# Loaded tiles with head rows 256 B apart, and their loads shared out over two issuing queues

## The chip, the cores and the metric

One core of a Trainium2 chip. The time is device microseconds of the whole program, a median over executions. A run also leaves a trace of one profiled execution; its span is about 2 us shorter than the time. Each execution lists the clock granted to TensorE; a run is called slow where it lies over 1.5% above the fastest of its kernel.

## The reference, cut to what matters

```python
# q, k, v, alpha: (4, 8, 768, 48) float32
for t in range(S):
    state = alpha[:, :, t, :, None] * state + np.einsum('bhd,bhe->bhde', k[:, :, t], v[:, :, t])
    y[:, :, t] = np.einsum('bhd,bhde->bhe', q[:, :, t], state)
x = y.transpose(0, 2, 1, 3).reshape(B * S, H * D)        # (3072, 384)
out = np.maximum(x @ w1, x @ w2) @ w_out                  # w1, w2: (384, 1024), w_out: (1024, 384)
```

The sequence is worked in 24 chunks (4 batches of 6) of 128 steps. A chunk needs four loads, alpha, k, q and v: 8 heads x 128 steps x 48 float32, so 1024 rows of 192 B (192 KB) each.

## The kernel before

```python
    ldp = ctx.enter_context(tc.tile_pool(name="ldp", bufs=8))
    ...
    def load(i):
        b, c = divmod(i, NCH)
        t = {}
        for name, src in (("af", alpha), ("kf", k), ("qf", q), ("vf", v)):
            t[name] = ldp.tile([128, H, D], FP32, tag=name, name=name)
            nc.sync.dma_start(out=t[name], in_=src[b, :, c * C : (c + 1) * C, :].rearrange("h p d -> p h d"))
        loads[i] = t

    load(0)
    load(1)
    ...                                        # w2f, wof, w1f: three weights of 1.5 MB, also nc.sync
    def gla(i):                                # one chunk; cut to the start of its chain
        nc.scalar.activation(out=lg[:, :, 0:D], in_=t["af"], func=ACTF.Ln)
        nc.gpsimd.tensor_copy(out=vd, in_=t["vf"])
        nc.tensor.matmul(csv, lhsT=mrec, rhs=lg[:, :, 0:D], start=True, stop=True)     # cs
        nc.scalar.activation(out=Em, in_=csv, func=ACTF.Exp, scale=-1.0)
        nc.scalar.activation(out=Ep, in_=csv, func=ACTF.Exp)
        nc.gpsimd.tensor_mul(out=kn[:, :, 0:D], in0=t["kf"], in1=Em)
        nc.vector.tensor_mul(out=qn[:, :, 0:D], in0=t["qf"], in1=Ep)
        ...                                    # transposes of kn, qn; qk, pp, pt, yp; xt by ScalarE
    for i in range(NI):
        if i + 2 < NI:
            load(i + 2)
        gla(i)
        if i == 1:
            weights()                          # ScalarE casts w2h; wq matmuls; w12
        if i % 2 == 1 and i // 2 - LAG >= 0:
            moe(i // 2 - LAG)                  # hp, gT, op; ScalarE evicts and issues the store
```

A scheduler orders the instructions of each engine when the program is built; ScalarE's 174 instructions, TensorE's 1544 matmuls and the issues of each queue come in the built order. It also hands out completion semaphores for the transfers: eight, in turn, whichever queue issues. The built program lets a transfer be issued only when the one eight places before it in that order has landed.

Of the kernel before, what the change touches and what calls it, by code (L numbers as in the profile page):

```python
# [9 lines left out]
FP32 = mybir.dt.float32  # L10
# [5 lines left out]
def kernel(  # L16
# [20 lines left out]
    nc = tc.nc  # L37
    B, H, S, D = q.shape
    C = 128
# [3 lines left out]
    P64 = 64  # L43
# [9 lines left out]
    ldp = ctx.enter_context(tc.tile_pool(name="ldp", bufs=8))  # L53
# [8 lines left out]
    def load(i):  # L62
        b, c = divmod(i, NCH)
        t = {}
        for name, src in (("af", alpha), ("kf", k), ("qf", q), ("vf", v)):
            t[name] = ldp.tile([128, H, D], FP32, tag=name, name=name)
            nc.sync.dma_start(out=t[name], in_=src[b, :, c * C : (c + 1) * C, :].rearrange("h p d -> p h d"))
        loads[i] = t

    load(0)  # L70
    load(1)
    w2f = wp.tile([128, ND, DFF], FP32)
    wof = wp.tile([128, NF, DM], FP32)
# [21 lines left out]
    for n in range(NB):  # L95
        for lst, nm in ((LG, "lg"), (QN, "qn"), (KN, "kn")):
            t = constp.tile([128, H, P64], FP16, name=f"{nm}{n}")
            nc.gpsimd.memset(t, 0.0)
            lst.append(t)
        t = constp.tile([128, 128 + H * VS], FP16, name=f"vp{n}")  # L100
# [3 lines left out]
    for n in range(3):  # L104
        t = constp.tile([128, 128 + HP * SS], FP16, name=f"sb{n}")
# [164 lines left out]
# [5 lines that stand above are left out]
            weights()  # L275
        if i % 2 == 1 and i // 2 - LAG >= 0:
            moe(i // 2 - LAG)
# [32 lines left out]
```

## Time and profile before

| | before |
|---|---|
| time, median | 187.52 us first; 188.06 with the run beside the changed kernel |
| TensorE busy, mean clock | 145.4 us of a 185.5 us span, 0.99 |
| ScalarE busy | 73.8 us (40%) |
| loads | 98304 packets of 192 B, all by SyncE |
| start of kn, chunks 0, 1, 2, 4, 7, 16, 23 | 10.3, 19.7, 32.4, 45.8, 63.8, 124.5, 168.6 us |

The start of kn (GpSimd's product of k and Em), read for each chunk from the timeline, is one number per chunk. From chunk 7 to 23 the pace before is (168.57 - 63.84)/16 = 6.55 us.

### The profile page before, as it was taken

The page shows a single profiled execution, that of the slowest core. Times are in us where ns is not written, and L with a number is a line of the kernel's source. Part 1 is how long each engine was busy: PE and PEld are TensorE (multiplying, and loading weights), DVE is VectorE, ACT ScalarE, POOL GpSimd, SP SyncE. Part 2 cuts the span into 40 slices and gives each one's busy share as a digit, 9 for nine tenths or more (in the row PEclk, how much of TensorE's full clock was granted, in tenths as well). Part 3 has the DMA queues.
Part 4 walks back from the last instruction along what each step waited for, and adds up shares of the span by engine and source line. Part 5 has one row for each costly group of instructions (what it writes and reads, how often), then busy time and mean ns, then how long its engine had stood idle before and what let it go on. Part 6 is the DMA issues. An engine that isn't in the chain of part 4 may idle for free. (4 is left out here: it accounts for less than half of the span.)

```text
span 185.5 us, 3954 instructions
## 1 busy us (share of the span) xinstructions
PE 145.4 (78%) x1544; PEld 101.6 (55%) x1544; DVE 102.6 (55%) x175; ACT 73.8 (40%) x175; POOL 75.9 (41%) x129
## 2 busy tenths in 40 slices
PE   0025779779887898896997878888878988969991
PEld 0024637556555666564675555566556665646760
DVE  4122765782764962955926757717649529559220
ACT  3306306525454616426344443252455163253331
POOL 8950730661464245436512543523633353355000
PEclk9999969999999999999999999999999999999999
DMA  6999999999699599996999994997920020020022
GB/s 119 189 351 378 370 189 169 196 187 168 163 201 216 114 191 206 190 189 142 185 161 221 205 208 105 194 189 157 169 88 0 4 85 2 5 85 0 4 85 85
DMA packets 104963, 28.57 MB, mean 154 GB/s; under 512 B 100080, under 2 KB 104176, under 8 KB 104944
## 3 DMA queue, kind: packets, MB, share of 16 engines
q1 hardware_dynamic: 101680, 23.60, 73.7%
q10 hardware_dynamic: 3264, 4.72, 7.4%
q8 instruction: 12, 0.20, 0.5%
q14 instruction: 7, 0.06, 0.1%
HBM read 23.59 MB, written 4.72 MB: 153 GB/s over the span
## 5 line engine op out<-in xcount | busy, mean ns | idle before, releaser
L171 POOL TENSOR_TENSOR kn<-kf,Em 128x384 f16<-128x384 f32 x24 | 23.9, 995 | 79.2 <-ACT Em L167 59.4
L260 PE MATMUL op<-wo,gT 128*128 128x384 f16 x192 | 40.6, 326 | 0.0
L246 PE MATMUL hp<-xt,w 128*128 128x256 f16 x288 | 38.9, 272 | 1.7 <-ACT xt L236 1.1
L221 DVE TENSOR_TENSOR pt<-pp,u 128x512 f16<-128x512 f32 x48 | 30.9, 685 | 6.2 <-PE pp L219 5.7
L253 DVE TENSOR_SCALAR gT<-hp 128x512 f16<-128x512 f32 x24 | 16.4, 684 | 24.1 <-PE hp L246 24.0
L246 PEld LDWEIGHTS <-w 128*128 128x128 f16 x288 | 26.1, 97 | 5.9 <-issue 3.2
L172 DVE TENSOR_TENSOR qn<-qf,Ep 128x384 f16<-128x384 f32 x24 | 21.1, 878 | 14.1 <-ACT Ep L168 10.6
L232 PE MATMUL yp<-pt,vp 128*128 128x128 f16 x240 | 26.3, 223 | 1.1 <-DVE pt L221 0.8
L177 PE MATMUL tp<-ident,kn 128*128 128x128 f16 x96 | 10.7, 229 | 19.5 <-POOL kn L171 19.5
L263 ACT COPY outs<-op 128x384 f32<-128x384 f32 x24 | 11.5, 480 | 33.6 <-PE op L260 33.5
L181 DVE COPY qk<-tp 128x1024 f16<-128x1024 f16 x24 | 16.5, 689 | 14.3 <-PE tp L177 12.9
L260 PEld LDWEIGHTS <-gT 128*128 128x128 f16 x192 | 16.9, 97 | 9.9 <-issue 1.8
L251 ACT ACTIVATE gT<-hp 128x512 f16<-128x512 f32 x24 | 14.4, 602 | 18.3 <-PE hp L246 18.2
L194 POOL TENSOR_TENSOR sb<-tm,dd 64x192 f16<-64x192 f32 x40 | 20.3, 506 | 2.9
L177 PEld LDWEIGHTS <-kn 128*128 128x128 f16 x96 | 6.1, 100 | 26.0 <-POOL kn L171 26.0
L232 PEld LDWEIGHTS <-vp 128*128 128x128 f16 x240 | 18.2, 100 | 3.3 <-issue 0.2
L167 ACT ACTIVATE Em<-cs 128x384 f32<-128x384 f32 x24 | 11.8, 493 | 18.8 <-PE cs L161 18.8
L236 ACT CAST xt<-yp 128x384 f16<-128x384 f32 x24 | 11.5, 479 | 18.6 <-PE yp L232 17.3
L154 POOL CAST vp<-vf 128x384 f16<-128x384 f32 x24 | 13.1, 550 | 12.6 <-PE yp L232 9.1
L232 PE MATMUL yp<-qk,sb 128*128 128x128 f16 x120 | 16.8, 222 | 1.0 <-POOL sb L194 1.0
L258 PE MATMUL op<-w2o,xt 128*128 128x384 f16 x72 | 16.9, 325 | 0.0
L209 DVE TENSOR_TENSOR tm<-kv,sb 64x192 f32<-64x192 f32 x32 | 11.3, 352 | 5.7 <-POOL sb L194 5.0
(46 smaller groups left out, 161.4 us busy)
## 6 DMA issues: line engine op xcount, KB each, us to landing
af<-in_alpha_dram SPq DMA_DIRECT2D x24, 192.0 KB, 4.5
kf<-in_k_dram SPq DMA_DIRECT2D x24, 192.0 KB, 4.6
qf<-in_q_dram SPq DMA_DIRECT2D x24, 192.0 KB, 4.6
vf<-in_v_dram SPq DMA_DIRECT2D x24, 192.0 KB, 4.6
out_dram<-outs ACTq DMA_DIRECT2D x12, 384.0 KB, 3.4
w2f<-in_moe_w_dram SPq DMA_DIRECT2D x1, 1536.0 KB, 7.3
wof<-in_moe_w_out_dram SPq DMA_DIRECT2D x1, 1536.0 KB, 10.5
w1f<-in_moe_w_dram SPq DMA_DIRECT2D x1, 1536.0 KB, 14.0
```

The source lines that it names most:

```text
L171: nc.gpsimd.tensor_mul(out=kn[:, :, 0:D], in0=t["kf"], in1=Em)
L172: nc.vector.tensor_mul(out=qn[:, :, 0:D], in0=t["qf"], in1=Ep)
L177: nc.tensor.transpose(tp[:, n, j, :], src[:, 2 * j : 2 * j + 2, :].rearrange("p h w -> p (h w)"), ident)
L181: nc.vector.tensor_copy(out=qk, in_=tp)
L194: nc.gpsimd.tensor_mul(out=sd[r, :, e], in0=tm[r], in1=dd[r, :].unsqueeze(2).to_broadcast([64, HP, D]))
L221: nc.vector.tensor_mul(out=pt[:, a], in0=pa[a], in1=u16.unsqueeze(1).to_broadcast([128, HP, C]))
L232: nc.tensor.matmul(yp[:, ds, :], lhsT=l, rhs=r, start=(n == 0), stop=(n == len(mms) - 1))
L246: nc.tensor.matmul(hp[:, n, :], lhsT=w12[:, ds, f * 128 : (f + 1) * 128], rhs=xt[:, ds].rearrange("p n t -> p (n t)"), start=(ds == 0), st ...
L251: nc.scalar.activation(out=gT[:, 2 * f2 : 2 * f2 + 2, :], in_=hp, func=ACTF.Relu)
L253: nc.vector.tensor_relu(out=gT[:, 2 * f2 : 2 * f2 + 2, :], in_=hp)
L258: nc.tensor.matmul(op, lhsT=xt[:, ds, n, :], rhs=w2o[:, ds, :], start=(ds == 0), stop=False)
L260: nc.tensor.matmul(op, lhsT=gT[:, f, n * C : (n + 1) * C], rhs=wo16[:, f, :], start=False, stop=(f == NF - 1))
```

## The change

Its intent: runs of 192 B that begin 256 B apart instead of packed, and half of the issues taken from SyncE.

```diff
-            t[name] = ldp.tile([128, H, D], FP32, tag=name, name=name)
-            nc.sync.dma_start(out=t[name], in_=src[b, :, c * C : (c + 1) * C, :].rearrange("h p d -> p h d"))
+            t[name] = ldp.tile([128, H, P64], FP32, tag=name, name=name)[:, :, 0:D]
+            eng = nc.sync if name in ("af", "qf") else nc.scalar
+            eng.dma_start(out=t[name], in_=src[b, :, c * C : (c + 1) * C, :].rearrange("h p d -> p h d"))
```

## The prediction

> **What bounds the kernel now.** I read the shares by slice first, then busy time by stretches of time, then the waits, and last the timeline of the first 32 us and the SyncE queue's own timeline. Busy time by stretch (columns: us, busy us of each engine with its instruction count, granted clock, mean share of the DMA engines, GB/s):
>
> ```profile
> 0.00:31.40 31.40, 14.72 (x128) 10.60 (x129) 13.96 (x27) 9.51 (x18) 16.27 (x28) 0.95 1.11 253
> 31.40:60.00 28.60, 24.16 (x272) 16.92 (x271) 16.29 (x28) 13.06 (x33) 13.76 (x24) 1.00 1.16 191
> 60.00:130.00 70.00, 60.75 (x670) 42.28 (x668) 43.17 (x74) 30.21 (x75) 27.98 (x47) 1.00 1.05 176
> ```
>
> After 31.4 us (the first expert matmul, hp) TensorE is busy 84 to 87% of the time, so its in-order stream sets the pace: 130.6 us of its 145.4 us lie there. The first 31.4 us hold only 14.7 us of its work; that ramp is where a faster load could pay. The DMA engines read as full almost throughout, which looks like a bound and is not one after the ramp: the SyncE queue pauses again and again (4 to 5 us at a time) for a store or a free buffer.
>
> The ramp, from the timeline, with the issue to landing time of two weights:
>
> ```profile
> w2f<-in_moe_w_dram SPq DMA_DIRECT2D x1, 1536.0 KB, 7.3
> wof<-in_moe_w_out_dram SPq DMA_DIRECT2D x1, 1536.0 KB, 10.5
> ...
> 7.58 0.96 SPq L75 DMA_DIRECT2D w2f<-in_moe_w_dram  x1
> 8.58 0.50 SPq L76 DMA_DIRECT2D wof<-in_moe_w_out_dram  x1
> 14.94 2.94 ACT L128 CAST w2h<-w2f 128x1024 f16<-128x1024 f32 x3 [6.31 <-DMA w2f<-in_moe_w_dram]
> 19.13 0.49 ACT L167 ACTIVATE Em<-cs 128x384 f32<-128x384 f32 x1 [1.25 <-PE cs L161]
> 20.64 3.07 POOL L133 CAST wo<-wof 128x3072 f16<-128x3072 f32 x1
> 27.86 0.48 ACT L141 CAST w2o<-wq 128x384 f16<-128x384 f32 x1 [6.63 <-PE wq L137]
> 31.44 1.25 PE L246 MATMUL hp<-xt,w 128*128 128x256 f16 x10
> ```
>
> Eight row loads, then w2f (landed 14.9), wof (19.1), w1f (23.1); ScalarE casts w2f, then does chunk 1's Em at 19.13; the product wq and w2o follow. So the ramp is made of DMA arrival and of ScalarE's program order.
>
> After the ramp ScalarE is not busy (40% of the span), but it starts every chunk:
>
> ```profile
> POOL kn L171 <- ACT Em L167: 59.4, 16, 8.0
> PE tp L177 <- POOL kn L171: 19.5, 21, 6.2
> ACT Em L167 <- PE cs L161: 18.8, 13, 2.9
> ```
>
> GpSimd's kn waits for Em in 16 of 24 chunks, TensorE waits for kn in 21 transposes. Em itself finds its matmul late in 13 chunks (1.45 us on average); in the other 11 it starts as soon as ScalarE is free. In those, anything put before Em on ScalarE moves the transposes.
>
> [...] But the built program puts these tiles at addresses that are 160 past a multiple of 256, so every 192-byte run would still cross a boundary (160 to 352); with the old pitch the offsets are 160, 96, 32 and 224, of which one in four does not cross. [...] The trace before has no aligned run to compare. [...]
>
> ```profile
> 87.39 0.37 SPq L67 DMA_DIRECT2D af<-in_alpha_dram  x1
> 87.85 0.53 SPq L67 DMA_DIRECT2D kf<-in_k_dram  x1
> 90.10 0.91 SPq L67 DMA_DIRECT2D af<-in_alpha_dram  x1
> 91.10 0.96 SPq L67 DMA_DIRECT2D kf<-in_k_dram  x1
> ```
>
> The first issue after a pause takes 0.37 us, later ones 0.9 to 1.0[...] (184 GB/s in 29 to 43 us, rows alone, against 378 in 10 to 23 us with the weights). [...]
>
> **The change part by part.**
> (1) Rows 256 B apart: the 98304 packets of 192 B stay; rate unchanged within a few per cent, 0 us. The engines' reads become eight runs of 48 elements; the outputs of Ln and kn already have such runs, so I take 0.
> (2) 48 of 96 loads leave SyncE, a queue with nothing else to do: worth nothing after the ramp, because loads are already chunks ahead.
> (3) 48 issues enter ScalarE's in-order stream. Each also waits for the landing of the transfer that used the same one of eight completion semaphores before. In the built order, k and v of chunks 2 and 3 stand before chunk 1's Ln; then w2h; then k4, v4, k5, v5, k6 stand between w2h and chunk 0's xt and chunk 1's Em. There v5 waits for v2 to land, k6 for wof.
>
> The ramp then. Four loads of SyncE and three of ScalarE share the DMA engines from 1.5 us at 1.0 us each: to 8.5. w2f (4.1 us of data at 378 GB/s) lands about 14.5 if the other ring takes little, about 19 if k2, v2, k3, v3 and v1 take their five microseconds in between; wof 19.5 or 23. In the first case the weights are near where they were, but k2 and v2 [...] land near 25, so k5 and v5, and behind them Em, wait to about 26; in the second Em waits for wof and its cs (which now stands behind five wq matmuls on TensorE) and comes at 27. Em of chunk 1 is thus 6 to 8 us later than 19.1. Not all is lost: w2h, wo and wq, which followed Em before, now run ahead of it, 24 wq matmuls of some 0.33 to 0.5 us, about 8 us with their waits. Alpha of chunk 2 is issued only when k3 has landed (near 26), lands near 30 and brings chunk 2's kn at about 34 to 35 instead of 32.4. I book +3.5 us (range +1 to +7).
>
> After the ramp: 32 issues (k and v of chunks 8 to 23) lie among the work of chunks 3 to 16. At 0.4 to 1.0 us each, say 0.6, that is 19 us of ScalarE time. About half falls into waits for TensorE that ScalarE has anyway (13 of 24 Em). The other half, 9.5 us, delays Em, xt or an eviction; TensorE has other matmuls in its stream and I take a third to a half of it as lost: +4 us (range +1 to +8). The waits for semaphores there should be met: each names a transfer some chunks older.
> Sum: 187.5 + 3.5 + 4 = 195.0.
>
> **The rivals.**
> (a) Alignment or a second ring quickens the rows. For: 184 GB/s is half of what the weights get. Against: base 160, and reads unchanged. A fifth more rate would save 1.5 us of the first eight loads and about 1 us on the next chunk, and nothing later: about 185 with no harm on ScalarE, 190 with some.
> (b) Hidden anyway: issues fall in ScalarE's idle 60%, and w2f, which is now fifth on SyncE, comes early; then 186 to 189. For: loads are far ahead in steady state. Against: five issues directly ahead of Em on the ramp.
> (c) The new order locks the two queues together: a ScalarE issue waits for a SyncE load that waits for a store or a buffer that ScalarE itself releases, each time for microseconds: 200 to 206. Against: the waits name transfers issued several chunks before.
>
> **Range and chances.** The main case is 191 to 199; (b) and part of (a) give the lower end, (c) the upper: 188 to 202. Faster by over 2% (under 183.8) needs (a) with no harm: 0.07. Within 2% (to 191.3): 0.25. Slower: 0.68.
>
> **What would show it.** Ramp: chunk 1's Em after 24 us, ScalarE waiting for a load's landing at v5 or k6; the first hp after 34 us. Steady: ScalarE-queue issues of 0.4 to 1.0 us, TensorE's wait for kn at the transposes well above 19.5 us, until about chunk 16, and the last chunks at their old pace (6.46 us: kn of chunk 4 starts at 45.79, of chunk 23 at 168.57). DMA: rows alone still at 175 to 195 GB/s. It is wrong if that rate rises over 215, if Em of chunk 1 comes before 22 us, or if the pace per chunk from chunk 4 to 16 stays at 6.5 us.

Where a cut is marked, a statement of how the hardware treats rows, issues or queues is left out that no trace or run of this case shows. The 1.0 us that the ramp takes for a load is 192 KB at the 184 GB/s of the trace (1.07 us). Three things can be measured now. Two queues share what the DMA engines move: with the pitch as built, rows alone go at 164 GB/s by two queues (changed) and at 163 by one (e1); only rows that cross no boundary gained from the second queue, 225 (e8) against 213 (e3). The engines read the padded tiles as fast as the packed ones, within 1%: kn takes 997 ns (median) against 996, Ln 535 against 530. And k2 and v2, issued near the weights, took 13.5 and 18.5 us to land in the changed kernel.

## The result, and the profile after

210.44 us (210.23 to 211.3, four fast runs) against 188.06 (187.39 to 189.44): ratio 1.1188, interval 1.1111 to 1.1265. Ratios here are the mean time of one kernel's fast runs over that of the other's fast runs of the same rounds, so not quite the ratio of the quoted medians. The direction was forecast, the size was not: 195.0 with 188 to 202.

First the start of kn in us:

| chunk | 0 | 1 | 2 | 3 | 4 | 7 | 8 | 16 | 23 |
|---|---|---|---|---|---|---|---|---|---|
| before | 10.3 | 19.7 | 32.4 | 37.0 | 45.8 | 63.8 | 71.4 | 124.5 | 168.6 |
| changed | 16.7 | 33.0 | 38.9 | 48.5 | 63.3 | 88.6 | 95.3 | 145.9 | 191.9 |
| later by | 6.5 | 13.3 | 6.5 | 11.5 | 17.5 | 24.8 | 23.9 | 21.3 | 23.4 |

All of the loss is there at chunk 7. From chunk 7 to 23 the pace is (191.93 - 88.62)/16 = 6.46 us, no slower than before, although 18 of the 32 issues for chunks 8 to 23 lie in that time on ScalarE. So two things have to be explained: the delay of chunk 1, and the growth from 6.5 to 24.8 us between chunks 2 and 7.

Busy time by stretch of the changed kernel (same columns as in the prediction):

```profile
0.00:38.00 38.00, 11.95 (x113) 8.37 (x114) 13.44 (x25) 9.37 (x18) 18.30 (x30) 1.00 1.25 230
38.00:90.00 52.00, 37.91 (x348) 26.96 (x346) 22.91 (x38) 16.76 (x43) 15.27 (x25) 0.84 1.45 177
90.00:136.00 46.00, 40.83 (x458) 29.21 (x456) 28.17 (x49) 20.37 (x50) 19.95 (x35) 1.00 1.09 161
```

In the middle stretch TensorE is busy 73% of the time at a granted clock of 0.84; before, it was 84 to 87% at 1.00. With the lower clock go longer matmuls (hp 285 ns on average against 272; 150.2 us busy in all, against 145.4), so part of the busy time here is not work gained.

The waits that answer to the three of before, and two new ones (who waited for whom, us in total, times, longest):

```profile
POOL kn L172 <- ACT Em L168: 46.2, 15, 6.8
PE tp L178 <- POOL kn L172: 16.4, 18, 3.3
ACT Em L168 <- PE cs L162: 14.0, 7, 2.9
ACT lg L154 <- DMA af<-in_alpha_dram: 9.5, 4, 4.8
ACT outs L264 <- DMA qf<-in_q_dram: 9.1, 2, 5.2
```

The first three did not grow; of TensorE's wait for kn I had forecast the opposite. ScalarE now waits for transfers, and one of these waits is odd: outs, the eviction of an expert result, reads no q. The timeline says what that is. First the start of ScalarE (start, us, engine or its queue, operation):

```profile
10.72 5.39 ACTq L68 DMA_DIRECT2D kf<-in_k_dram  x1
16.16 0.49 ACT L168 ACTIVATE Em<-cs 128x384 f32<-128x384 f32 x1 [4.94 <-issue]
16.25 6.64 ACTq L68 DMA_DIRECT2D vf<-in_v_dram  x1
22.94 0.52 ACT L154 ACTIVATE lg<-af 128x384 f16<-128x384 f32 x1 [5.83 <-issue]
23.36 2.92 ACT L129 CAST w2h<-w2f 128x1024 f16<-128x1024 f32 x3
32.46 0.50 ACT L168 ACTIVATE Em<-cs 128x384 f32<-128x384 f32 x1
```

The issues of k and v of chunk 3 last 5.39 and 6.64 us, while the weights are moved (w2f lands at 16.50, wof at 21.90). Em of chunk 0 comes at 16.16 (before: 5.13), Ln of chunk 1 at 22.94 (8.11), and w2h at 23.36, although w2f landed at 16.5 (issued 4.70, 11.8 us to landing). On SyncE the same stretch had cost nothing: the timeline before has a load's issue that lasts 6.22 us, on a queue with nothing else to do:

```profile
13.07 6.22 SPq L67 DMA_DIRECT2D kf<-in_k_dram  x1
```

The waits of Ln (lg) come next, 9.5 us in all. In ScalarE's new order Ln of chunks 4 and 5 stands before Em of chunk 3, and ScalarE stood there until their alpha had landed (43.85 and 47.45 us), 4.8 and 2.7 us. That is alpha arriving late, and it comes ahead of the waits that are shown next.

Then ScalarE and SyncE around chunk 4, merged in order of time:

```profile
49.28 1.14 SPq L68 DMA_DIRECT2D qf<-in_q_dram  x1
54.13 1.09 SPq L68 DMA_DIRECT2D qf<-in_q_dram  x1
57.11 0.38 ACTq L68 DMA_DIRECT2D kf<-in_k_dram  x1
57.52 0.48 ACT L237 CAST xt<-yp 128x384 f16<-128x384 f32 x1 [3.23 <-DMA qf<-in_q_dram]
61.88 0.38 ACTq L68 DMA_DIRECT2D kf<-in_k_dram  x1
62.30 0.48 ACT L264 COPY outs<-op 128x384 f32<-128x384 f32 x1 [3.92 <-DMA qf<-in_q_dram]
62.68 0.50 ACT L168 ACTIVATE Em<-cs 128x384 f32<-128x384 f32 x1
```

The Em at 62.68 is chunk 4's. In ScalarE's order the issues of k10 and k11 stand before it. By the shared semaphores k10 may be issued when q7 (issued 49.28) has landed, and k11 when q8 (issued 54.13) has: each takes nearly 8 us to land, and ScalarE stands there. The bracket's "DMA qf" is the wait of the issue ahead of the named instruction, not of xt or outs themselves. Computing chunk 4 has become dependent on q of chunk 8 having arrived. The trace bears the semaphores out: q7 lands at 57.03 and k10 is issued at 57.11, q8 lands at 61.80 and k11 is issued at 61.88.

This can be counted. Up to the start of chunk 7's kn the changed kernel has issued 63 loads, the kernel before 44. In the stretch from 29 to 43 us rows alone move at 164 GB/s; before, at 184. First the changed kernel, then the one before:

```profile
29.00:43.00 14.00, 10.03 (x99) 6.88 (x97) 11.09 (x16) 4.44 (x12) 6.55 (x10) 0.89 1.51 164
```

```profile
29.00:43.00 14.00, 12.05 (x129) 8.19 (x126) 9.35 (x16) 6.09 (x15) 6.23 (x11) 1.00 1.25 184
```

A load of 196608 B then takes 1.20 us, and the three weights, 4.72 MB at the 378 GB/s of the stretch from 10 to 23 us before, 12.5 us. 12.5 + 63 x 1.20 = 88.1 us, an estimate from these numbers; chunk 7's kn starts at 88.6. As 63 is read at that very moment, the sum says only that the loads ran without a pause up to there. That the computing waits for them is what the waits above and the experiments have to show. So the theory: **under the split ScalarE cannot reach chunk n until loads some four to eight chunks ahead have gone through, so the computing runs at the rate of the rows until the buffers are full; and the pitch lowers that rate, from 184 to 164 GB/s, with every row now across a multiple of 256 B instead of three of four.** That the rate goes with the crossings is shown under e12, where four layouts stand side by side. In the expectations, theory A is its first half, with late arrival counted in; the second half and the count were put together as the runs came in (63 first stands in the expectation of e9). Rivals: the pitch does the harm alone (B); two rings, that is two issuing queues at once, lower the rate (C); the late arrival of alpha and q, not ScalarE's standing still, is what costs (D). One more rival has to be kept in mind: the split changes the order in which the scheduler builds TensorE's instructions, too.

### The profile page after: what moved, and what is told of

Its sections match the earlier page's. It is cut to its first block, busy times and chain, and to the rows that moved or that the text cites. A ratio compares the mean times of both kernels' runs of the same rounds, so it can differ in the third digit from the quotient of the medians.

```text
span 208.6 us, 3951 instructions
## 1 busy us (share of the span) xinstructions
PE 150.2 (72%) x1544; PEld 105.6 (51%) x1544; DVE 104.1 (50%) x175; ACT 73.0 (35%) x175; POOL 77.5 (37%) x129
## 3 DMA queue, kind: packets, MB, share of 16 engines
HBM read 23.59 MB, written 4.72 MB: 136 GB/s over the span
## 5 line engine op out<-in xcount | busy, mean ns | idle before, releaser
L172 POOL TENSOR_TENSOR kn<-kf,Em 128x384 f16<-128x384 f32 x24 | 24.4, 1017 | 74.0 <-ACT Em L168 46.2
L247 PE MATMUL hp<-xt,w 128*128 128x256 f16 x288 | 40.9, 285 | 5.4 <-ACT outs L264 2.6
L173 DVE TENSOR_TENSOR qn<-qf,Ep 128x384 f16<-128x384 f32 x24 | 21.8, 910 | 34.0 <-ACT Ep L169 19.9
L247 PEld LDWEIGHTS <-w 128*128 128x128 f16 x288 | 27.7, 102 | 10.3 <-issue 6.7
L254 DVE TENSOR_SCALAR gT<-hp 128x512 f16<-128x512 f32 x24 | 16.5, 686 | 25.3 <-PE hp L247 25.2
L264 ACT COPY outs<-op 128x384 f32<-128x384 f32 x24 | 11.6, 483 | 37.8 <-PE op L261 28.6
L178 PE MATMUL tp<-ident,kn 128*128 128x128 f16 x96 | 10.9, 236 | 16.4 <-POOL kn L172 16.4
L154 ACT ACTIVATE lg<-af 128x384 f16<-128x384 f32 x24 | 12.9, 536 | 24.0 <-DMA af<-in_alpha_dram 9.5
L168 ACT ACTIVATE Em<-cs 128x384 f32<-128x384 f32 x24 | 11.8, 494 | 25.9 <-PE cs L162 14.0
L178 PEld LDWEIGHTS <-kn 128*128 128x128 f16 x96 | 6.6, 105 | 21.4 <-POOL kn L172 21.4
## 6 DMA issues: line engine op xcount, KB each, us to landing
af<-in_alpha_dram SPq DMA_DIRECT2D x24, 192.0 KB, 7.0
kf<-in_k_dram ACTq DMA_DIRECT2D x24, 192.0 KB, 6.0
qf<-in_q_dram SPq DMA_DIRECT2D x24, 192.0 KB, 6.4
vf<-in_v_dram ACTq DMA_DIRECT2D x24, 192.0 KB, 6.4
w2f<-in_moe_w_dram SPq DMA_DIRECT2D x1, 1536.0 KB, 11.8
```

Of the source, the lines that this page charges most:

```text
L178: nc.tensor.transpose(tp[:, n, j, :], src[:, 2 * j : 2 * j + 2, :].rearrange("p h w -> p (h w)"), ident)
L247: nc.tensor.matmul(hp[:, n, :], lhsT=w12[:, ds, f * 128 : (f + 1) * 128], rhs=xt[:, ds].rearrange("p n t -> p (n t)"), start=(ds == 0), st ...
L254: nc.vector.tensor_relu(out=gT[:, 2 * f2 : 2 * f2 + 2, :], in_=hp)
```

## The experiments

Twelve kernels ran, all correct. k and v by ScalarE is called the split. "Rows" is the rate in the stretch from 29 to 43 us.

| run | pitch, first row past a multiple of 256 | on ScalarE: k, v of chunks | time us | ratio (interval) | rows GB/s | kn of chunk 7 |
|---|---|---|---|---|---|---|
| before | packed, 160 | none | 187.5 to 189.1 | 1 | 184 | 63.8 |
| changed | 256, 160 | all | 210.4 | 1.119 (1.111 to 1.127) | 164 | 88.6 |
| e1 | 256, 160 | none | 189.7 | 1.006 (0.999 to 1.013) | 163 | 66.3 |
| e2 | packed, 160 | all | 201.3 | 1.068 (1.060 to 1.076) | 187 | 80.4 |
| e3 | 256, 0 | none | 187.5 | 0.994 (0.985 to 1.003) | 213 | 64.5 |
| e4 | packed, 160 | 8 to 23 | 188.4 | 1.000 (0.993 to 1.008) | 179 | 67.7 |
| e5 | packed, 160 | 0 to 3 | 195.1 | 1.032 (1.030 to 1.034) | 181 | 71.4 |
| e6 | packed, 160 | 4 to 7 | 194.3 (fast runs 191.8, 193.5) | 1.019 (1.013 to 1.025), unclear at 2% | 170 (slow run) | 71.3 (slow run) |
| e7 | packed, 160 | none, order of e2 | 192.0 (one fast run) | none given | 183 (slow run) | 71.4 (slow run) |
| e8 | 256, 0 | all | 187.9 | 0.997 (0.990 to 1.003) | 225 | 66.9 |
| e9 | 256, 160, 3 buffers | all | 198.5 | 1.054 (1.050 to 1.057) | 164 | 72.9 |
| e10 | 256, 0 | 0 and 1 | 184.2 | 0.978 (0.976 to 0.979) | 205 | 60.3 |
| e11 | 256, 0, weights earlier | none | 185.7 | 0.985 (0.981 to 0.988) | 208 | 61.9 |
| e12 | packed, 0 | none | 186.5 (one look; before 188.6) | none given | 201 | 63.0 |

The kernel before was timed with each call, on that call's chip: 187.8 for e1 to e4, 189.1 for e5 to e8, 188.6 for e9 to e12.

The traces show which kernels can be compared without the rival of the order. The changed kernel, e2 and e8 have the same order of instructions on every engine, but for the pad's memset in e8; so have the kernel before, e1, e3 and e12. In e4 to e7 and in e10 and e11 TensorE's order differs from that before, in e9 from that of the changed kernel.

### e1 to e4: the parts alone

e1, the pitch alone:

```diff
-            t[name] = ldp.tile([128, H, D], FP32, tag=name, name=name)
+            t[name] = ldp.tile([128, H, P64], FP32, tag=name, name=name)[:, :, 0:D]
```

> Rows 256 B apart, all loads still on SyncE (built order identical to before). Theory A (the ScalarE queue's in-order waits for loads and the order in which loads arrive make the loss): 187 to 190 us, because the pitch touches neither. Theory B (the 256 B pitch lowers the rate of the rows, seen as 164 GB/s after against about 185 before, and the ramp is bound by it): rows alone at 165 to 170 GB/s in the first 45 us, time 193 to 205. Theory C (two rings lower the rate): rate as before, 187 to 189.

e2, the split alone:

```diff
-            nc.sync.dma_start(out=t[name], in_=src[b, :, c * C : (c + 1) * C, :].rearrange("h p d -> p h d"))
+            eng = nc.sync if name in ("af", "qf") else nc.scalar
+            eng.dma_start(out=t[name], in_=src[b, :, c * C : (c + 1) * C, :].rearrange("h p d -> p h d"))
```

> k and v on the ScalarE queue, rows packed as before. Theory A: 206 to 212 us, the ramp as in the changed kernel (chunk 7's kn near 85 us or later). Theory B: 188 to 197, because the row rate is back at about 185 GB/s. Theory C: about 210 with rows at 164 GB/s. If A holds and B adds a part, 203 to 207 with rows above 175 GB/s.

e3, e1 with its tiles moved to a multiple of 256 B:

```diff
+    padp = ctx.enter_context(tc.tile_pool(name="padp", bufs=1))
+    pad = padp.tile([128, 24], FP32, name="pad")
+    nc.vector.memset(pad, 0.0)
     ldp = ctx.enter_context(tc.tile_pool(name="ldp", bufs=8))
```

> All loads on SyncE, rows 256 B apart, and the tiles moved by 96 B so that every row starts on a multiple of 256 B and none crosses one. If the boundaries on the side of the on-chip memory count, rows alone run faster than the 184 GB/s of before (200 or more) and the ramp shortens by 1 to 2 us: 185.5 to 187. If they don't count: 184 GB/s and 187 to 189.

e4, the split for late chunks only:

```diff
+            eng = nc.scalar if name in ("kf", "vf") and i >= 8 else nc.sync
+            ...                                    # eng.dma_start, as in e2
```

> Packed rows; the first eight chunks' loads all on SyncE, k and v of chunks 8 to 23 on the ScalarE queue. Theory A, with the whole loss in the ramp: 187 to 190 us, although ScalarE issues 32 loads among its work. What I predicted for this part (+4 us): 190 to 193. If the loss needs only ScalarE issues anywhere: above 198.

e1: the rows fall to 163 GB/s, as B said, and yet the time hardly moves. The same stretch from 29 to 43 us of e1, and then of e3:

```profile
29.00:43.00 14.00, 12.04 (x118) 8.64 (x117) 8.73 (x14) 6.52 (x16) 6.25 (x11) 0.91 1.28 163
```

```profile
29.00:43.00 14.00, 12.04 (x127) 8.33 (x125) 9.37 (x16) 5.74 (x15) 6.24 (x11) 0.97 1.08 213
```

TensorE has 12.04 us of work in both, although the rows move at 163 GB/s in one and 213 in the other. With all loads on SyncE the computing is not bound by them after the ramp, as the prediction said; B as the whole cause is out. And the place of the tile counts: 96 B turn 163 into 213 GB/s. But the ramp of e3 is not 1 to 2 us shorter, as I had expected (chunk 7's kn at 64.5, before 63.8).

e2: 201.3 us, in none of the ranges that I gave, with rows at 187 GB/s:

```profile
29.00:43.00 14.00, 10.13 (x108) 7.39 (x108) 11.00 (x17) 5.25 (x14) 6.76 (x10) 0.88 1.44 187
```

Two rings do not lower the rate (187 against 184), so C is out; the split alone costs 12 to 14 us. By the estimate above, 12.5 + 63 x 1.05 = 78.7 us; chunk 7's kn came at 80.4. The parts are not additive (1.006 and 1.068 alone, 1.119 together), as it must be if the split makes the computing wait for a given number of loads and the pitch sets how long each takes.

e4: 32 issues of loads among ScalarE's work and no loss, 1.000. My +4 us for that part was nothing: in the trace of e4 the 32 issues take 17.5 us in all, near the 19 that I had reckoned, but nothing is lost by them.

### e5 to e8: where in the ramp, and which mechanism

e5 and e6, the split for chunks 0 to 3 and for 4 to 7:

```diff
+            eng = nc.scalar if name in ("kf", "vf") and i < 4 else nc.sync            # e5
+            eng = nc.scalar if name in ("kf", "vf") and 4 <= i < 8 else nc.sync       # e6
```

> Packed rows; k and v of chunks 0 to 3 alone on the ScalarE queue. In the split kernel the issues of k3 and v3 stood on ScalarE for 5.2 and 6.4 us behind the weights and put chunk 1's kn back by 11.7 us, chunk 2's by 5.0. If that blocked issue is one part of the loss and the later chunks' the other: chunk 1's kn at 26 to 30 us, then the old pace; 190 to 193.5 us. If the first part alone makes the whole loss: about 201. If none of it: 188.

> Packed rows; k and v of chunks 4 to 7 alone on the ScalarE queue; chunks 0 to 3 as before. Now no issue stands behind the weights ahead of Em of chunk 1. If the rest of the loss (chunks 3 to 8, +11 us in the split kernel) comes from ScalarE waiting, before its own work, for loads of chunks ahead: 190 to 197. If it needs the delayed start: 187 to 189.

e7, every load on SyncE, but in the one order in which the build of the split kernel places its first 35 transfers (its queues ran ahead of each other: in e2's trace wof was issued before v2, and w1f before k3, so in e7 they come later):

```diff
+    for s in ("a0 q0 k0 a1 v0 q1 k1 w2 v1 k2 v2 k3 wo v3 w1 k4 v4 k5 v5 a2 k6 q2 a3 q3 v6 a4 q4 k7 a5 q5 v7 a6 q6 a7 q7").split():
+        ...                                    # each by nc.sync.dma_start
```

> Packed rows, every load on SyncE, but the first eight chunks' loads and the weights issued in the one order in which the split kernel's two queues issue them (k and v of up to chunk 5 ahead of alpha of chunk 2). It has the late arrival of alpha and q without ScalarE's part. If late arrival makes the loss: 198 to 202 us. If ScalarE standing still at its issues makes it: only chunk 2 comes some 4 us later (alpha 2 is the 20th transfer: 8 us of rows + 12.5 of weights + 9 of rows), 190 to 193.

e8, the changed kernel with the pad of e3 in front of its tiles:

> The changed kernel as it stands, with its tiles moved by 96 B so that no row crosses a 256 B boundary. Pitch and split together cost 22.4 us, apart 1 to 2 and 13.5, so under the split the row rate must count far more than without it. If so: rows alone above 200 GB/s in 29 to 43 us and 193 to 199 us. If the rate is not what makes the difference between 201 and 210: 205 or more.

e5 costs 3.2% and puts chunk 1's kn at 30.6 (before: 19.7), above the range that I gave for it, as is the time; after chunk 4 it keeps the old pace ((176.40 - 53.39)/19 = 6.47 us). e6 leaves chunk 1 where it was (19.67) and costs 1.9% by its two fast runs. Together they are 5.1% against the 6.8% of e2. But e6 does not test what it was meant to test: in its trace each of the eight issues on ScalarE comes 4.7 us or more after the transfer eight before it has landed. They hold ScalarE up once, by their own length (1.8 us, at Ln of chunk 3), and never by a landing. What changed as well is TensorE's order (cs of chunk 3 starts at 39.58 instead of 35.91, behind more hp and op matmuls), so the cause of its 1.9% stays open. Two of the four runs of e6, the profiled one among them, were slow, so I take no duration of the ramp but chunk 1's as a measure.

e7 has the late alpha and q without ScalarE's part. Three of its four runs were slow; the one fast run is 192.0 us, against 189.1 for the kernel before on the same chip. The slow ones took 195.3 to 197.3. Its expectation for D was 198 to 202. So arrival order costs some 3 us of e2's 13, by one run and with TensorE in another order; that ScalarE's standing still has the larger part is likely, and not shown by this run.

e8 is the sharpest test, and it surprised me: the whole change, with only its tiles moved by 96 B, costs nothing (0.997). I had expected 193 to 199. Its rows:

```profile
29.00:43.00 14.00, 10.10 (x136) 7.67 (x135) 11.52 (x19) 7.05 (x19) 8.69 (x14) 1.00 1.13 225
```

63 loads before chunk 7's kn again, as in e2: 12.5 + 63 x 0.874 = 67.5 us, seen 66.9. ScalarE still stands at the issues of k3 and v3, for 4.65 and 5.78 us, and chunk 1's kn is at 28.6, but by chunk 7 it is 3.1 us behind the kernel before, and at chunk 23, 0.8. Its ScalarE finds q7 and q8 landed when it comes to k10 and k11, and its trace shows no wait of ScalarE for alpha. The three kernels with the same built order and three row rates (164, 187, 225 GB/s) put chunk 7 at 88.6, 80.4 and 66.9 us against estimates of 88.1, 78.7 and 67.5. As the order is the same and the loss is gone, TensorE's new order is not what costs by itself: the loss needs the split and rows at 187 GB/s or less together.

### e9 to e12: depth of the run ahead, a better version, and the boundaries

e9, the changed kernel with fewer buffers:

```diff
-    ldp = ctx.enter_context(tc.tile_pool(name="ldp", bufs=8))
+    ldp = ctx.enter_context(tc.tile_pool(name="ldp", bufs=3))
```

> The changed kernel, unaligned pitch and all, with three buffers for each loaded tile instead of eight, so that no load can stand more than three chunks ahead of its use. In the changed kernel 63 loads are issued before chunk 7's kn, and that moment is when they have been moved: 12.5 us of weights and 63 x 1.20 us at 164 GB/s = 88 us (seen: 88.6). With three buffers it can be no more than 40: 12.5 + 48 = 60.5 us, under the pace of the computing. If the loss is ScalarE standing at the issues of loads far ahead: chunk 7's kn at 66 to 72, time 190 to 196 us with rows still at 164 GB/s. If the slow rows or ScalarE's issues do harm at any depth: 204 or more.

e10, e3 with the split for the first two chunks:

```diff
+            eng = nc.scalar if name in ("kf", "vf") and i < 2 else nc.sync
```

> Try at a version that beats both: rows 256 B apart and starting on multiples of 256 B, and only k and v of chunks 0 and 1 on the ScalarE queue, which is idle then, so that w2f comes fifth on SyncE. Rows alone 205 to 250 GB/s; chunk 1's kn some 1 to 2 us before 19.7; 185 to 187.5 us. If the ramp is set by GpSimd's zeroing and the order of ScalarE rather than by arrival: 187 to 188.

e11, e3 with load(1) moved behind w2f and wof:

```diff
     load(0)
-    load(1)
     ...                                        # w2f, wof
+    load(1)
     nc.sync.dma_start(out=w1f, in_=moe_w1.rearrange("(s p) f -> p s f", p=128))
```

> Aligned pitch, all loads on SyncE, and w2f and wof issued between chunk 0's loads and chunk 1's. w2f lands near 11 instead of 15 and wof near 15 instead of 19, chunk 1 near 19: if the ramp waits for weights, 184 to 186.5 us; if for chunk 1: 187 to 190.

e12, the kernel before with the pad of e3:

> The kernel before with its loaded tiles moved by 96 B: packed rows that start at 0, 192, 128 and 64 past a multiple of 256, so two of four cross a boundary, against three of four before, four of four with the pitch alone, none with the aligned pitch. If the crossings set the rate, rows alone (29 to 43 us) lie between the 184 GB/s of before and the 213 of the aligned pitch: 193 to 203. Time 186 to 188.5.

e9: taking away five of eight buffers makes the changed kernel faster, 210.4 to 198.5 us, with rows still at 164 GB/s. Chunk 7's kn is at 72.9 instead of 88.6, just above the 66 to 72 that I expected. From chunk 4 to chunk 7 it stays 8.4 to 9.3 us behind the kernel before, where the changed kernel goes from 17.5 to 24.8; and after k2 none of ScalarE's load issues starts right on the landing that it depends on, as seven do in the changed kernel. TensorE's order changed with the buffers, so this is a weaker test than e8. The time lies above my 190 to 196, and not in the ramp alone: from chunk 7 to 23 its pace is (179.91 - 72.86)/16 = 6.69 us, 2.3 us in sum more than before. I ran no kernel with three buffers and all loads on SyncE, so whether that is the buffers or ScalarE's issues is open.

e10 beats both kernels: 184.2 us, ratio 0.978. Its issues on ScalarE end before there is anything to do there (v1 at 3.93 for 0.86 us), and the ramp:

```profile
12.71 2.94 ACT L132 CAST w2h<-w2f 128x1024 f16<-128x1024 f32 x3 [5.35 <-DMA w2f<-in_moe_w_dram]
19.98 0.49 ACT L171 ACTIVATE Em<-cs 128x384 f32<-128x384 f32 x1 [4.33 <-PE cs L165]
24.13 0.48 ACT L145 CAST w2o<-wq 128x384 f16<-128x384 f32 x1 [1.96 <-PE wq L141]
```

w2h starts 2.2 us earlier than before (12.71 against 14.94) and w2o 3.7 us earlier (24.13 against 27.86); chunk 7's kn is 3.5 us earlier. Not as I expected, chunk 1's kn is 0.9 us later: the ramp seems to have waited for weights, not for chunk 1. e11 says the same from the other side: weights ahead of chunk 1's loads, 0.985 (less than the 2% that is called faster, but clear of noise), chunk 7's kn 2.0 us earlier. The aligned pitch that both have gave 0.994 in e3; what TensorE's changed order adds in either, no run tells.

e12: packed rows at another base, 201 GB/s, within what I had given:

```profile
29.00:43.00 14.00, 12.04 (x133) 8.37 (x132) 9.91 (x16) 5.61 (x14) 6.24 (x11) 1.00 1.03 201
```

The four layouts that were on SyncE alone:

| layout | rows that cross a 256 B boundary | GB/s |
|---|---|---|
| 256 B pitch from 160 (e1) | 4 of 4 | 163 |
| packed from 160 (before) | 3 of 4 | 184 |
| packed from 0 (e12) | 2 of 4 | 201 |
| 256 B pitch from 0 (e3) | 0 of 4 | 213 |

The fewer rows cross, the higher the rate: 21 GB/s from four to three of four, 17 from three to two, but only 12 from two to none. There something other than the crossings takes over: from 35 to 41 us, where SyncE issues without a pause, e12 and e3 are equal (209 GB/s; before 187, e1 164). It is not all that the DMA engines can do with such rows, for e8 moved them at 225 with two issuing queues, and at 248 from 41 to 50 us. What it is, and why the rate goes with the crossings, no run here takes apart.

## Why the prediction was wrong

**Right**: what bounds the kernel before (e1 and e3 move the row rate by 50 GB/s and the time by about 1%); no gain in rate from a second ring for rows as built (e2: 187 against 184 GB/s; for aligned rows there was one, 225 in e8 against 213 in e3); the addresses, that the pitch as built makes every row cross a boundary; the sign; that alpha of chunk 2 would be issued only when k3 had landed (27.98, issued at 28.00). Right by luck: chunk 1's Em came after 24 us, at 32.46, but not behind a wait for v2 or wof to land. v5 and k6 followed the issues before them without a gap; it was the length of the issues, k3 to k6, that held it up. Of the other signs, the first hp came at 45.2 us (forecast: after 34) and the pace from chunk 4 to 16 was 6.88 us, but TensorE's wait for kn fell to 16.4 us, and the row rate left its 175 to 195 GB/s. One reading was a little off: in the last 55 us before, TensorE is busy 82%, not 84 to 87%.

**Wrong, the ramp's term.** "I book +3.5 us (range +1 to +7)": chunk 7 was 24.8 us late. Three steps failed in it; the third I had put under the time after the ramp, but its waits come from chunk 4 on.

- *"rate unchanged within a few per cent, 0 us"*. 184 became 164 GB/s. I had the addresses, three rows of four across a multiple of 256 B before and all four after, and booked nothing for them; no trace that I had then compared two layouts. The fall is 11%. Alone it costs about 1 us (e1, not clear of noise); under the split it is the difference between 201 and 210.
- *"Four loads of SyncE and three of ScalarE share the DMA engines"*, and the steps after it. They follow the data and give the issues on ScalarE no time of their own (elsewhere I took 0.4 to 1.0 us). The issues of k3 and v3 behind the weights lasted 5.39 and 6.64 us, and chunk 1 was 13.3 us late, not 6 to 8. The trace before had the like (6.22 us on SyncE), and I did not read it as a property of the queue that would move to ScalarE. The w2h, wo and wq that were to run ahead came late with it (w2h 8.4 us later than before). e5 has this part: 3.2%, with issues of 5.18 and 6.69 us.
- *"The waits for semaphores there should be met: each names a transfer some chunks older."* Older in the scheduler's order, yes, but younger than the computing: k11, before chunk 4's Em, waits for q8. It is the first half of my rival (c), which I gave 200 to 206 and dismissed with that sentence. The second half did not happen: up to k11 no SyncE load waited for a store or a buffer; q7 and q8 took nearly 8 us because other loads were on the way. With three buffers the waits are gone (e9), and faster rows make them harmless (e8).

**Wrong, the term after the ramp.** "+4 us (range +1 to +8)" was for the length of the issues, and that cost 0. e4 has these 32 issues alone, at 1.000, and the changed kernel's pace from chunk 7 on is 6.46 us. With buffers full, each issue is short (0.37 to 0.4 us for most of them); that it falls where ScalarE waits anyway is likely, not shown.

**Open.** The changed kernel's clock was 0.956 to 0.967 in its four runs, e8's 0.977 to 1.000 and the kernel before's about 0.98 to 0.99; its matmuls were busy 4.8 us longer. Whether a TensorE that runs in fits brings the lower clock, or the clock adds to the delay, no run separates; but 4.8 us is the most that the longer matmuls can add to a loss of 22.

## What to carry to other kernels

An engine that computes should issue only transfers that are due while it has nothing to do: its issue stands in line with its work, can last for microseconds behind large transfers (5.39 and 6.64 us here; on SyncE before, 0.37 for the first load after a pause and 0.9 to 1.0 a few loads later), and waits for whatever transfers the semaphores tie it to, so that a deep prefetch turns from a reserve into a condition (here 63 loads before chunk 7). For short rows look up the address that the tile gets, not only its pitch: 96 B of padding moved the row rate from 163 to 213 GB/s, and the whole change from 210 to 188 us. What paid was to bring the weights forward: by giving the idle start of a second queue four loads (184.2 us), or by issuing two weights before chunk 1's loads (185.7 us).
